# Layer two's first-mixer GELUs of tiles 4 to 11 in the tanh form, ranks and rates set anew, and queues left in the planner's order, in a two-layer attention and mixer kernel

## The chip, the cores and the metric

The kernel runs on one core of a Trainium2 chip. Times are device microseconds of that core. The time before is 1024.59 us, the median of three runs (1024.34 to 1025.14). TensorE (PE), VectorE (DVE), ScalarE (ACT), GpSimd (POOL) and the DMA queue of SyncE (SP) each work through a list of instructions in a fixed order and wait for each other by semaphores.

## The reference

The input is 2048 rows of 448 numbers, in bfloat16. Block A is attention with 16 heads of 28 dimensions, block B a token-shifting mixer and an MLP. Each stands behind a layer norm, and the pair runs twice with the same weights (cut to what matters):

```
def _A_ref(x, wqkv, wo):
    qkv = (x @ wqkv) split into q, k, v of 16 heads
    p = softmax(q @ k^T * 28 ** -0.5)
    return (p @ v) @ wo
def _B_ref(x, w1, w2, w3, w4):
    h = gelu_tanh(layernorm(x) @ w1)
    hs = (h, its quarters shifted by 1, -1, 2, -2 rows) @ w2
    x1 = x + hs
    return x1 + gelu_tanh(layernorm(x1) @ w3) @ w4
x = x + A(layernorm(x)); x = x + B(layernorm(x))
x = x + A(layernorm(x)); x = x + B(layernorm(x))
```

## The kernel before

**Tiles and chunks.** The 2048 rows are 16 tiles of 128. For queries, a layer has five chunks: tiles 0-3, 4-7, 8-11, 12-13 and 14-15. The heads are worked four at a time, in four groups. The MLP of block B runs over five groups of tiles: 0-2, 3-6, 7-10, 11-12 and 13-15.

**The stream of exponentials.** `t_scores` (L1775) writes score blocks of 128 keys by 512 (or two of 256) into PSUM with L1654. Two or three blocks make a unit; units take turns on banks 0-2 and 3-4, so PE can be two units ahead of ACT. `t_exp` (L1877) turns a whole unit into probabilities by one ACTIVATE of 1536 or 1024 columns (L1892), and `t_pv` (L1904) multiplies them with v (L1050). A share of the blocks doesn't go to ACT: `d_first` and `d_chain` (L1734, L1747) compute the exponential on DVE with five instructions (L1736, L1763, L1765, L1767, L1770). `R_RATE` and `D_RATE` say how large this share is in each stretch.

**The first mixer.** `t_mixA` (L2093) multiplies a chunk with w1, and DVE brings its four groups into `hT` (L2128). Its GELU is done in one of two forms. In the tanh form (`tanh_gelu`, L2152) each group takes a square (L2156, on POOL or DVE), a product on DVE (L2157), a Tanh of 512 columns on ACT (L2158) and a second product on DVE (L2159). In the wide form one ACTIVATE with the GELU function takes all four groups at once (L2140, 2048 columns). The table `PAIR` chooses the wide form for a chunk and names the group of tiles with whose MLP GELU (`t_mixB`, L2339) it shares a stay of ACT in the GELU table. Both then wait for each other:

```
PAIR = {(0, 12): 7, (1, 4): 0, (1, 8): 3}
...
once = (L, tiles[0]) in PAIR and not direct
...
for f in range(14):
    yield ("wait", ("h2", L, PAIR[L, t0], f))
...
for (L_, c0), g0 in sorted(PAIR.items()):
    if (L_, g0) == (L, tiles[0]) and not direct:
        for grp in range(4):
            yield ("wait", ("hz", L, c0, grp))
```

**Who sets the order.** All of this is written as generators that offer operations to a planner (`Sched.run`, L618). It holds a cost for each operation, chooses what an engine takes next by readiness and by `RANK`, and puts dummy matmuls on the identity (L2385) into PE's gaps. `WIN`, `TARGET` and `LWIN` say how densely, and `W_POS` and `Q_LEAD` when weights and queries are loaded. The result is one list for each engine. In the kernel before, this list isn't the last word: `Plan.rearranged` (L274) takes 370 pairs from `MOVES` (L19), each of which puts one operation behind another on the same engine, and `WEAVE` (L67) says how the five lists are interleaved for the recording of dependences. `FILL_MORE` (L172) lengthens six stretches of dummy matmuls.

**Start and end.** Before the first score, PE transposes the normalised tiles 0 to 3 (L1283, recorded as `ps<-ident,xn`), DVE copies them (L1290), and PE projects keys and queries (L1059). Beside it ACT packs weights (L1188) and squares them (L1200); PE sums those squares (L1050 on `ones_bf`) for the bound under the softmax. After the last exponential, what remains is the MLP of tiles 7 to 15 and the last chunk's mixer, and the GELUs then come straight out of PSUM (L2313, L2123).

Of the kernel before, what the change touches and what calls it, by code (L numbers as in the profile page):

```python
# [2496 lines left out]
```

## Time and profile before

| | |
|---|---|
| median of three runs | 1024.59 us (1024.34 to 1025.14) |
| span of the profiled execution, first to last instruction | 1022.4 us, its clock 1.000 |
| ACT busy | 981.4 us, 894 instructions |
| PE busy, and of that dummy matmuls on the identity | 973.8 us, 150.1 us (3524 of 16283) |
| DVE busy | 811.0 us |
| POOL busy | 292.3 us |
| ACT table loads | 14 of 1.283 us |

The span leaves out what lies before the first and behind the last instruction; to the median of the runs it is 2.2 us. Busy time on PE overlaps (four matmuls run side by side in column groups, their ends are modelled), and successive ACTIVATEs overlap by a little, so the cost of one on ACT is the distance to the start of the next rather than its own length.

### The profile page before, as it was taken

The page shows a single profiled execution, that of the slowest core. Times are in us where ns is not written, and L with a number is a line of the kernel's source. Part 1 is how long each engine was busy: PE and PEld are TensorE (multiplying, and loading weights), DVE is VectorE, ACT ScalarE, POOL GpSimd, SP SyncE. Part 2 cuts the span into 40 slices and gives each one's busy share as a digit, 9 for nine tenths or more (in the row PEclk, how much of TensorE's full clock was granted, in tenths as well). Part 3 has the DMA queues.
Part 4 walks back from the last instruction along what each step waited for, and adds up shares of the span by engine and source line. Part 5 has one row for each costly group of instructions (what it writes and reads, how often), then busy time and mean ns, then how long its engine had stood idle before and what let it go on. Part 6 is the DMA issues. An engine that isn't in the chain of part 4 may idle for free.

```text
span 1022.4 us, 36170 instructions
## 1 busy us (share of the span) xinstructions
PE 973.8 (95%) x16283; PEld 412.9 (40%) x16285; DVE 811.0 (79%) x1572; ACT 981.4 (96%) x894; POOL 292.3 (29%) x462
## 2 busy tenths in 40 slices
PE   8999999999999999999999999999999999999998
PEld 4332443443433254333433443433433433454565
DVE  8777999989888958876877868688898589866651
ACT  8999999999999999999999999999999999999942
POOL 3312021531453016252325112012624120532230
PEclk9999999999999999999999999999999999999999
DMA  4643413320321013131131024423302020121101
GB/s 126 161 111 117 119 45 79 53 39 23 76 61 28 13 37 96 23 48 34 48 111 38 33 69 134 141 66 99 65 25 37 17 68 16 31 57 31 26 12 33
DMA packets 99394, 62.57 MB, mean 61 GB/s; under 512 B 68712, under 2 KB 88552, under 8 KB 99240
## 3 DMA queue, kind: packets, MB, share of 16 engines
q1 hardware_dynamic: 99240, 60.27, 23.6%
q8 instruction: 127, 2.08, 0.9%
q14 instruction: 27, 0.22, 0.1%
HBM read 28.16 MB, written 16.76 MB: 44 GB/s over the span
## 4 chain that ended last, share of the span: by engine, by line
ACT 71%; PE 23%; DVE 4%; DMA 1%; issue 1%; DVEq 0%
ACT PT L1892 65%; PE ps L1059 14%; PE ps L1654 5%; PE ps L1050 4%; ACT h2T L2339 2%; ACT fb L2158 1%; PE ps L2385 1%; ACT L1892 1%; DVE PD L1770 0%; ACT hT L2140 0%; DVE h2T L2317 0%; DMA xT<-xn 0%; ACT L2339 0%; DMA obf<-in_A_x_dram 0%; DVE yd L1736 0%
## 5 line engine op out<-in xcount | busy, mean ns | idle before, releaser
L1892 ACT ACTIVATE PT<-ps 128x1024 bf16<-128x1024 f32 (+1 forms) x782 | 887.3, 1333 | 2.9 <-PE ps L1654 2.1
L1654 PE MATMUL ps<-qT,kT 32*128 32x512 bf16 (+1 forms) x2304 | 269.8, 335 | 24.2 <-ACT PT L1892 18.4
L1050 PE MATMUL ps<-PT,vaug 128*32 128x512 bf16 (+1 forms) x2420 | 246.1, 341 | 0.7 <-ACT PT L1892 0.2
L1059 PE MATMUL ps<-xT,w 128*32 128x512 bf16 (+4 forms) x2656 | 177.9, 344 | 4.2 <-DVE h2T L2317 2.2
L1654 PEld LDWEIGHTS ps<-qT,kT 32*128 32x128 bf16 x2304 | 69.7, 91 | 256.0 <-ACT PT L1892 227.0
L2385 PE MATMUL ps<-ident 128*32 128x256 bf16 x3524 | 150.1, 276 | 1.8 <-POOL ident L1144 1.5
L2385 PEld LDWEIGHTS ps<-ident 128*32 128x32 bf16 x3524 | 98.9, 97 | 28.5 <-issue 11.9
L1050 PEld LDWEIGHTS ps<-PT,vaug 128*32 128x32 bf16 x2420 | 74.0, 95 | 89.4 <-issue 71.0
L1999 POOL TENSOR_TENSOR otn<-ub,fb 128x512 bf16<-128x512 f32 (+1 forms) x31 | 34.7, 1120 | 210.3 <-DMA fb<-rscr 202.9
L1736 DVE TENSOR_SCALAR yd<-ps 128x512 int32<-128x512 f32 x109 | 74.6, 685 | 22.8 <-PE ps L1654 21.7
L1059 PEld LDWEIGHTS ps<-xT,w 128*32 128x32 bf16 (+1 forms) x2656 | 69.2, 95 | 56.7 <-issue 25.0
L1763 DVE SCALAR_TENSOR_TENSOR fb<-yd 128x512 f32<-128x512 uint16 x109 | 78.5, 724 | 0.8
L1765 DVE SCALAR_TENSOR_TENSOR fb<-fb,yd 128x512 f32<-128x512 f32 x109 | 77.9, 717 | 0.7
L1770 DVE SCALAR_TENSOR_TENSOR PD<-yd,PD 128x512 int16<-128x512 int16 x109 | 75.9, 698 | 1.6
L1059 PE MATMUL ps<-w,h2T 128*32 128x448 bf16 x1120 | 75.4, 355 | 1.1 <-ACT h2T L2339 1.0
L2317 DVE CAST h2T<-ps 128x512 bf16<-128x512 f32 (+1 forms) x70 | 44.4, 635 | 16.2 <-PE ps L1059 15.0
L1392 POOL TENSOR_TENSOR sq<-qT 128x512 bf16<-128x512 bf16 x24 | 28.5, 1190 | 96.2 <-DVE qT L1451 93.4
L1392 POOL TENSOR_TENSOR sq<-kT 128x512 bf16<-128x512 bf16 (+2 forms) x32 | 30.4, 950 | 83.0 <-DVE kT L1406 79.9
L1767 DVE TENSOR_SCALAR PD<-fb 128x512 bf16<-128x512 f32 x109 | 49.6, 456 | 1.0
L1059 PE MATMUL ps<-xT,wk_pad 128*32 128x512 bf16 (+2 forms) x576 | 47.6, 359 | 0.7 <-DVE kT L1406 0.3
L1654 PE MATMUL ps<-wk_pad,kT 32*128 32x512 bf16 x256 | 39.6, 384 | 4.6 <-ACT PT L1892 4.0
L1059 PE MATMUL ps<-xT,wq_pad 128*32 128x512 bf16 x512 | 43.2, 382 | 0.5 <-issue 0.5
(189 smaller groups left out, 1195.9 us busy)
## 6 DMA issues: line engine op xcount, KB each, us to landing
uscr<-ub SPq DMA_DIRECT2D x28, 256.0 KB
ub<-uscr SPq DMA_DIRECT2D x28, 256.0 KB, 6.8
fb<-rscr SPq DMA_DIRECT2D x24, 256.0 KB
xnd<-xn SPq DMA_DIRECT2D x28, 128.0 KB, 2.3
xd<-x_res SPq DMA_DIRECT2D x16, 224.0 KB, 2.1
x_res<-xd SPq DMA_DIRECT2D x16, 224.0 KB, 4.2
w<-in_B_w_dram SPq DMA_DIRECT2D x5, 448.0 KB, 6.0
obf<-in_A_x_dram SPq DMA_DIRECT2D x16, 112.0 KB
```

Of the source, the lines that this page charges most:

```text
L1050: return lambda e: e.matmul(out=out, lhsT=lhsT, rhs=rhs, start=start, stop=stop, **kw)
L1059: r.append(e.matmul(out=out[c:c + w, :], lhsT=lhsT[:, c:c + w], rhs=rhs, start=start, stop=stop, tile_position=(0, c)))
L1392: return both("sq", 0.15 + NW * 0.0018, 0.07 + NW * 0.00104, lambda e: e.tensor_tensor(out=sq[:, si, 0:NW], in0=src, in1=src, op=ALU.mult) ...
L1654: yield op("pe", (0.005 + NW * 0.00042) / nc_, lambda e, i=i, kc=kc, j=j, g=g, qt=qt, a=a, NW=NW, bank=bank: e.matmul(out=ps[:, bank, i * ...
L1736: yield op("dve", c_ps(512), lambda e: e.tensor_scalar(out=y, in0=ps[:, bi(bank), :], scalar1=SCALE * L2E * FS, scalar2=-126.0 * FS, op0=A ...
L1763: yield op(D_[0][0], D_[0][1], lambda e: e.scalar_tensor_tensor(out=q, in0=lo, scalar=E2 / E3 * FS, in1=lo, op0=ALU.add, op1=ALU.mult), re ...
L1765: yield op(D_[1][0], D_[1][1], lambda e: e.scalar_tensor_tensor(out=q, in0=q, scalar=E1 / E3 * FS * FS, in1=lo, op0=ALU.add, op1=ALU.mult) ...
L1767: yield op(D_[2][0], D_[2][1], lambda e: e.tensor_scalar(out=pdt, in0=q, scalar1=E3 / FS ** 3, scalar2=E0, op0=ALU.mult, op1=ALU.add), rea ...
L1770: yield op(D_[3][0], D_[3][1], lambda e: e.scalar_tensor_tensor(out=pdt.bitcast(I16), in0=hi, scalar=128.0, in1=pdt.bitcast(I16), op0=ALU. ...
L1892: yield op("act", 0.069 + n * w * 0.000833, lambda e, bk=bk, s0=s0, n=n, w=w: e.activation(out=PT[:, s0:s0 + n, 0:w], in_=ps[:, bk[0]:bk[0 ...
L2317: ev = op("dve", c_ps(m * NW), lambda e, hr=hr, pv=pv: e.tensor_copy(out=hr, in_=pv), reads=[("ps", bi(b))], writes=hk, touch=[b])
L2385: return [e.matmul(out=ps[32 * c:32 * c + 32, bi(b), 0:256].rearrange("p (a n) -> p a n", n=128), lhsT=ident[:, 32 * c:32 * c + 32], rhs=i ...
```

## The change

`MOVES`, `WEAVE` and `FILL_MORE` become empty, so each engine gets its instructions in the order of the planner. `PAIR` loses its two entries of layer two: chunks 4-7 and 8-11 take the tanh form, and the wide GELUs of the groups of tiles 0-2 and 3-6 wait for them no more. The planner's other tables get new numbers.

```
-MOVES = (
-    (94, 115), (95, 94), (96, 95), (97, 96), (125, 118), (128, 125), (130, 134), (238, 231), (244, 238), (245, 244),
...
-WEAVE = (
-    "vdvvvvsgdvgvvdtgtvgdtvtgdtsgtgvdvtvttdvtvvtdttvtvdgtgtdvtvtdtstvvtdgsvtttdtsgtttttstttsvttttvstgtttttttvtttttt",
...
-FILL_MORE = (
-    (2714, 4), (2725, 9), (3749, 15), (5548, 4), (5564, 4), (9810, 14),
-)
+MOVES = ()
+WEAVE = ()
+
+FILL_MORE = ()
...
-DPRIO = 3.5
+DPRIO = 4.797
...
-RHI = 7
+RHI = 9
...
-DTH = 0.4
-XSHUT = (8, 83)
+DTH = 0.396
+XSHUT = (10, 78)
...
-DDTH = 1.3
+DDTH = 1.889
...
-Q_LEAD = {(0, 0): 0, (0, 1): 4, (0, 2): 45, (0, 3): 11, (1, 0): 18, (1, 1): 12, (1, 2): 4, (1, 3): 26}
+Q_LEAD = {(0, 0): 0, (0, 1): 8, (0, 2): 54, (0, 3): 11, (1, 0): 7, (1, 1): 17, (1, 2): 8, (1, 3): 35}
...
-Sched.TARGET = 0.695
+Sched.TARGET = 0.78
 Sched.LOW = 0
-Sched.WIN = 1.582
-Sched.LWIN = 3.6
+Sched.WIN = 1.535
+Sched.LWIN = 3.231
...
-W_POS = (6, 9, 17, 5, 5, 5, 25, 21)
-V_FIRST = 1.366
-K_FIRST = (0.756, 0.932, 1.363)
-Q_FIRST = (0.531, 1.956, 2.405)
+W_POS = (3, 7, 17, 5, 3, 14, 29, 16)
+V_FIRST = 1.113
+K_FIRST = (0.617, 0.789, 1.032)
+Q_FIRST = (0.3, 1.262, 2.77)
...
-PAIR = {(0, 12): 7, (1, 4): 0, (1, 8): 3}
+PAIR = {(0, 12): 7}
```

`RANK`, `R_RATE`, `D_RATE` and `PE_NORM` change in the same way, number by number. What this makes of the built program, counted in it:

| | before | changed |
|---|---|---|
| exponentials on ACT (L1892), and blocks of 512 columns in them | 782, 1938 | 781, 1940 |
| exponentials on DVE, chains of five | 110 | 108 |
| GELU of 2048 columns (L2140) | 2 | 0 |
| Tanh of 512 columns of the first mixer (L2158 on `hT`) | 16 | 24 |
| products of the tanh form on DVE, 512 columns (L2157 and L2159 on `hT`) | 16 and 16 | 24 and 24 |
| squares of the tanh form, 512 columns (L2156 on `hT`), DVE and POOL | 5 and 11 | 10 and 14 |
| ACT table loads | 14 | 14 |
| dummy matmuls on the identity | 3524 | 3652 |

More of the change, by code (lines that the diff above doesn't have):

```diff
@@ L172 @@
-FILL_MORE = (
-    (2714, 4), (2725, 9), (3749, 15), (5548, 4), (5564, 4), (9810, 14),
-)
+MOVES = ()
+WEAVE = ()
+FILL_MORE = ()
 class _Op:
@@ L771 @@
 PVB = 2
-DPRIO = 3.5
+DPRIO = 4.797
 DST = [('dve', 0.6), ('dve', 0.6), ('dve', 0.34), ('dve', 0.6)]
 DSEG = 1
-R_RATE = {0: 0.072, 1: 0.054, 2: 0.185, 3: 0.027, 4: 0.084, 5: 0.015, 6: 0.079, 7: 0.153, 8: 0.15, 9: 0.2, 10: 0.068, 11: 0.141, 13: 0.013, 14: 0.093, 15: 0.07, 16: 0.166, 17: 0.069, 18: 0.125, 19: 0.035, 20: 0.104, 21: 0.101, 22: 0.2, 24: 0.083, 25: 0.131, 26: 0.05, 27: 0.2, 28: 0.031, 29: 0.146, 30: 0.13, 31: 0.151, 32: 0.106, 34: 0.194, 35: 0.032, 36: 0.048, 37: 0.159, 38: 0.2, 39: 0.152, 40: 0.017, 41: 0.066, 42: 0.126, 43: 0.193, 44: 0.161, 45: 0.152, 46: 0.185, 47: 0.071, 48: 0.099, 49: 0.145, 50: 0.04, 51: 0.149, 52: 0.2, 53: 0.035, 54: 0.081, 55: 0.109, 56: 0.113, 57: 0.2, 58: 0.094, 59: 0.173, 60: 0.07, 61: 0.036, 62: 0.03, 63: 0.022}
+R_RATE = {0: 0.033, 1: 0.054, 2: 0.181, 3: 0.053, 4: 0.132, 5: 0.035, 6: 0.019, 7: 0.153, 8: 0.189, 9: 0.2, 10: 0.068, 11: 0.076, 13: 0.052, 14: 0.093, 15: 0.07, 17: 0.183, 18: 0.2, 19: 0.035, 20: 0.156, 22: 0.2, 24: 0.189, 27: 0.198, 28: 0.031, 29: 0.159, 30: 0.051, 31: 0.121, 32: 0.091, 34: 0.2, 37: 0.11, 38: 0.044, 39: 0.188, 40: 0.017, 42: 0.126, 43: 0.078, 44: 0.155, 46: 0.2, 47: 0.059, 48: 0.099, 49: 0.145, 50: 0.04, 52: 0.2, 53: 0.025, 54: 0.081, 55: 0.113, 56: 0.128, 57: 0.078, 59: 0.042, 60: 0.07, 61: 0.067, 62: 0.035, 63: 0.022, 12: 0.017, 23: 0.166, 41: 0.019, 25: 0.031}
 RLO = 5
-RHI = 7
+RHI = 9
 RPRIO = 1
 DWIN = 2
-DTH = 0.4
-XSHUT = (8, 83)
+DTH = 0.396
+XSHUT = (10, 78)
 DLO = 6
@@ L784 @@
 DPK = 2
-DDTH = 1.3
+DDTH = 1.889
 UPRIO = 2
 UWAIT = 1
-RANK = {('q', 0, 1): 1.458, ('q', 0, 2): 3.2, ('q', 0, 3): 2.4, ('q', 1, 0): 2.293, ('q', 1, 1): 2.021, ('q', 1, 2): 3.05, ('q', 1, 3): 1.801, ('b', 0, 0): 2.202, ('b', 0, 1): 3.2, ('b', 0, 2): 2.582, ('b', 0, 3): 3.2, ('b', 0, 4): 1, ('b', 1, 0): 2.957, ('b', 1, 1): 2.988, ('b', 1, 2): 3.1, ('b', 1, 3): 2.326, ('b', 1, 4): 2.625, ('a', 0, 0): 1, ('a', 0, 1): 1.329, ('a', 0, 2): 2.222, ('a', 0, 3): 1.987, ('a', 0, 4): 1.487, ('a', 1, 0): 2.563, ('a', 1, 1): 2.326, ('a', 1, 2): 1, ('a', 1, 3): 1.418, ('a', 1, 4): 1.12, ('k', 0, 1): 2.363, ('k', 0, 2): 3.2, ('k', 0, 3): 3.2, ('k', 1, 0): 2.011, ('k', 1, 1): 2.88, ('k', 1, 2): 2.852, ('k', 1, 3): 2.609, ('k', 1, 4): 1, ('c', 0, 0): 1, ('c', 0, 1): 2.803, ('c', 0, 2): 1.953, ('c', 0, 3): 1.333, ('c', 0, 4): 2.22, ('c', 1, 0): 2.575, ('c', 1, 1): 2.272, ('c', 1, 2): 2.13, ('c', 1, 3): 1, ('c', 1, 4): 1, ('w', 0, 0): 3.2, ('w', 0, 1): 2.902, ('w', 0, 2): 1.222, ('w', 0, 3): 2.911, ('w', 0, 4): 2.596, ('w', 1, 0): 2.665, ('w', 1, 1): 3.2, ('w', 1, 2): 3.125, ('w', 1, 3): 3.2, ('w', 1, 4): 2.29, ('o', 0, 0): 1.812, ('o', 0, 1): 1.176, ('o', 0, 2): 1.382, ('o', 0, 3): 3.2, ('o', 0, 4): 1, ('o', 1, 0): 2.392, ('o', 1, 1): 3.077, ('o', 1, 2): 1.372, ('o', 1, 3): 1.772, ('o', 1, 4): 1.234, ('v', 0, 1): 2.98, ('v', 0, 2): 1.671, ('v', 0, 3): 3.2, ('v', 1, 0): 1.713, ('v', 1, 1): 2.534, ('v', 1, 2): 2.146, ('v', 1, 3): 2.138, ('v', 1, 4): 3.2, ('l', 1, 0): 2.708, ('l', 1, 1): 2.19, ('l', 1, 2): 1.408, ('l', 1, 3): 3.2, ('l', 1, 4): 2.671, ('t', 0, 0): 2.601, ('t', 0, 1): 2.03, ('t', 0, 2): 2.728, ('t', 0, 3): 3.07, ('t', 0, 4): 2.082, ('t', 1, 0): 1.898, ('t', 1, 1): 2.494, ('t', 1, 2): 2.877, ('t', 1, 3): 2.854, ('t', 1, 4): 1, ('m', 0, 0): 1, ('m', 0, 1): 1.667, ('m', 0, 2): 2.633, ('m', 0, 3): 2.857, ('m', 0, 4): 1.917, ('m', 1, 0): 2.491, ('m', 1, 1): 2.982, ('m', 1, 2): 1.289, ('m', 1, 3): 2.323, ('m', 1, 4): 2.62, ('e', 0, 0): 0.6, ('e', 0, 1): 0.666, ('e', 0, 2): 1.865, ('e', 0, 3): 1.412, ('e', 0, 4): 0.716, ('e', 1, 0): 0.703, ('e', 1, 1): 2.839, ('e', 1, 2): 0.6, ('e', 1, 3): 0.722, ('e', 1, 4): 0.679, ('n', 0, 0): 1.011, ('n', 0, 1): 1.107, ('n', 0, 2): 1.382, ('n', 0, 3): 1.706, ('n', 0, 4): 1.167, ('n', 1, 0): 0.6, ('n', 1, 1): 1.548, ('n', 1, 2): 1.666, ('n', 1, 3): 1.653, ('n', 1, 4): 1.663}
@@ L789 @@
-Q_LEAD = {(0, 0): 0, (0, 1): 4, (0, 2): 45, (0, 3): 11, (1, 0): 18, (1, 1): 12, (1, 2): 4, (1, 3): 26}
-D_RATE = {1: 0.194, 3: 0.3, 4: 0.033, 6: 0.118, 7: 0.195, 8: 0.122, 9: 0.124, 10: 0.166, 11: 0.072, 12: 0.023, 13: 0.025, 14: 0.281, 15: 0.015, 16: 0.293, 17: 0.033, 18: 0.288, 19: 0.106, 20: 0.056, 21: 0.3, 22: 0.057, 23: 0.097, 24: 0.185, 25: 0.22, 26: 0.255, 27: 0.117, 28: 0.3, 29: 0.081, 30: 0.058, 32: 0.151, 33: 0.011, 34: 0.268, 35: 0.165, 37: 0.3, 38: 0.218, 39: 0.061, 40: 0.025, 41: 0.299, 42: 0.272, 43: 0.122, 44: 0.137, 45: 0.032, 46: 0.014, 47: 0.256, 48: 0.021, 49: 0.021, 50: 0.107, 51: 0.074, 52: 0.129, 54: 0.155, 55: 0.3, 56: 0.3, 57: 0.162, 58: 0.227, 59: 0.149, 60: 0.061, 61: 0.154, 62: 0.079, 63: 0.137}
@@ L791 @@
-PE_NORM = {(0, 0): 0, (0, 1): 0, (0, 2): 0, (0, 3): 0, (0, 4): 0, (1, 0): 0, (1, 1): 0, (1, 2): 0, (1, 3): 0, (1, 4): 1}
+RANK = {('q', 0, 1): 1.529, ('q', 0, 2): 3.2, ('q', 0, 3): 2.4, ('q', 1, 0): 2.293, ('q', 1, 1): 1.947, ('q', 1, 2): 3.05, ('q', 1, 3): 1.147, ('b', 0, 0): 2.071, ('b', 0, 1): 3.2, ('b', 0, 2): 2.649, ('b', 0, 3): 3.061, ('b', 0, 4): 1, ('b', 1, 0): 1.526, ('b', 1, 1): 2.988, ('b', 1, 2): 2.904, ('b', 1, 3): 2.119, ('b', 1, 4): 2.559, ('a', 0, 0): 1, ('a', 0, 1): 1.329, ('a', 0, 2): 3.102, ('a', 0, 3): 2.09, ('a', 0, 4): 1.56, ('a', 1, 0): 1.126, ('a', 1, 1): 1.363, ('a', 1, 2): 2.002, ('a', 1, 3): 2.451, ('a', 1, 4): 2.131, ('k', 0, 1): 2.252, ('k', 0, 2): 3.031, ('k', 0, 3): 3.2, ('k', 1, 0): 2.054, ('k', 1, 1): 2.905, ('k', 1, 2): 2.853, ('k', 1, 3): 2.609, ('k', 1, 4): 1, ('c', 0, 0): 1, ('c', 0, 1): 3.043, ('c', 0, 2): 1.986, ('c', 0, 3): 2.534, ('c', 0, 4): 2.249, ('c', 1, 0): 2.575, ('c', 1, 1): 2.044, ('c', 1, 2): 1.058, ('c', 1, 3): 1.094, ('c', 1, 4): 2.116, ('w', 0, 0): 1.569, ('w', 0, 1): 2.708, ('w', 0, 2): 1.222, ('w', 0, 3): 2.916, ('w', 0, 4): 2.085, ('w', 1, 0): 2.665, ('w', 1, 1): 2.176, ('w', 1, 2): 2.488, ('w', 1, 3): 3.2, ('w', 1, 4): 1.727, ('o', 0, 0): 1.814, ('o', 0, 1): 1.459, ('o', 0, 2): 1.07, ('o', 0, 3): 3.2, ('o', 0, 4): 1, ('o', 1, 0): 1.731, ('o', 1, 1): 3.012, ('o', 1, 2): 1.574, ('o', 1, 3): 2.146, ('o', 1, 4): 1, ('v', 0, 1): 2.98, ('v', 0, 2): 1.671, ('v', 0, 3): 3.2, ('v', 1, 0): 1.981, ('v', 1, 1): 2.421, ('v', 1, 2): 2.144, ('v', 1, 3): 1.392, ('v', 1, 4): 2.544, ('l', 1, 0): 2.708, ('l', 1, 1): 2.342, ('l', 1, 2): 1.152, ('l', 1, 3): 3.087, ('l', 1, 4): 1.775, ('t', 0, 0): 3.183, ('t', 0, 1): 2.03, ('t', 0, 2): 2.728, ('t', 0, 3): 3.024, ('t', 0, 4): 2.654, ('t', 1, 0): 2.807, ('t', 1, 1): 2.762, ('t', 1, 2): 3.151, ('t', 1, 3): 3.099, ('t', 1, 4): 2.905, ('m', 0, 0): 1, ('m', 0, 1): 1, ('m', 0, 2): 2.363, ('m', 0, 3): 3.156, ('m', 0, 4): 2.922, ('m', 1, 0): 2.491, ('m', 1, 1): 3.076, ('m', 1, 2): 2.965, ('m', 1, 3): 2.551, ('m', 1, 4): 3.051, ('e', 0, 0): 0.6, ('e', 0, 1): 0.783, ('e', 0, 2): 1.865, ('e', 0, 3): 1.464, ('e', 0, 4): 0.734, ('e', 1, 0): 0.703, ('e', 1, 1): 2.839, ('e', 1, 2): 2.154, ('e', 1, 3): 0.919, ('e', 1, 4): 0.6, ('n', 0, 0): 1.115, ('n', 0, 1): 1.448, ('n', 0, 2): 1.476, ('n', 0, 3): 1.706, ('n', 0, 4): 1.117, ('n', 1, 0): 0.694, ('n', 1, 1): 1.555, ('n', 1, 2): 1.698, ('n', 1, 3): 1.629, ('n', 1, 4): 1.621}
@@ new lines @@
+Q_LEAD = {(0, 0): 0, (0, 1): 8, (0, 2): 54, (0, 3): 11, (1, 0): 7, (1, 1): 17, (1, 2): 8, (1, 3): 35}
+D_RATE = {1: 0.194, 3: 0.3, 6: 0.118, 7: 0.143, 8: 0.18, 9: 0.124, 10: 0.237, 11: 0.072, 13: 0.025, 14: 0.3, 16: 0.206, 18: 0.288, 20: 0.056, 21: 0.255, 22: 0.131, 23: 0.2, 24: 0.194, 25: 0.22, 26: 0.143, 27: 0.15, 28: 0.045, 29: 0.074, 30: 0.041, 32: 0.151, 33: 0.216, 35: 0.022, 37: 0.3, 38: 0.062, 39: 0.061, 40: 0.025, 41: 0.206, 42: 0.3, 43: 0.093, 44: 0.163, 46: 0.014, 47: 0.03, 48: 0.021, 49: 0.021, 50: 0.107, 51: 0.074, 52: 0.213, 54: 0.155, 55: 0.245, 56: 0.3, 57: 0.179, 58: 0.228, 59: 0.149, 60: 0.057, 61: 0.133, 62: 0.157, 63: 0.145, 5: 0.093, 19: 0.03, 53: 0.279}
@@ L792 @@
+PE_NORM = {(0, 0): 0, (0, 1): 0, (0, 2): 0, (0, 3): 0, (0, 4): 0, (1, 0): 0, (1, 1): 0, (1, 2): 0, (1, 3): 0, (1, 4): 2}
 TANHW = {(0, 0): 0, (0, 3): 0, (0, 7): 0, (0, 11): 1, (0, 13): 0, (1, 0): 0, (1, 3): 0, (1, 7): 0, (1, 11): 0, (1, 13): 0}
 Sched.AGED = 0
-Sched.TARGET = 0.695
+Sched.TARGET = 0.78
 Sched.LOW = 0
-Sched.WIN = 1.582
-Sched.LWIN = 3.6
+Sched.WIN = 1.535
+Sched.LWIN = 3.231
 GSL = 0
@@ L814 @@
 COLD = 6.0
-Sched.DOUBT2 = {"dma": 1.5, "pool": 0.2, "dve": 0.5, "act": 0.5, "pe": 0.0}
+Sched.DOUBT2 = {'dma': 1.5, 'pool': 0.2, 'dve': 0.5, 'act': 0.5, 'pe': 0}
 Sched.EARLY = 0.1
-Sched.DOUBT = {"dma": 0.8, "pool": 0.6, "dve": 0.05, "act": 0.05}
+Sched.DOUBT = {'dma': 0.8, 'pool': 0.6, 'dve': 0.05, 'act': 0.05}
+Sched.LCRED = 0.3
 def PENORM(L, ch, g):
```

102 lines of the change are left out of this document (removed), and 45 rows, old and new, of the table MOVES.

## The prediction

> **What bounds the kernel now.** I read the page first, then the chain of waits, then busy time by stage.
>
> ```profile
> span 1022.4 us, 36170 instructions
> PE 973.8 (95%) x16283; PEld 412.9 (40%) x16285; DVE 811.0 (79%) x1572; ACT 981.4 (96%) x894; POOL 292.3 (29%) x462
> ACT 71%; PE 23%; DVE 4%; DMA 1%; issue 1%; DVEq 0%
> ```
>
> Two engines look full. Which one sets the end depends on the stage, so the next view gives busy time in five windows of us; the first number after each is its length, and the brackets count instructions.
>
> ```profile
> 27.00:968.00 941.00, 898.86 (x14709) 369.15 (x14709) 768.67 (x1454) 937.16 (x833) 275.95 (x421) 1.00 0.25 62
> 666.00:760.00 94.00, 89.34 (x1386) 35.62 (x1382) 80.96 (x139) 93.35 (x88) 30.07 (x41) 1.00 0.27 66
> 760.00:830.00 70.00, 66.20 (x1045) 26.84 (x1045) 53.45 (x106) 69.72 (x59) 24.40 (x45) 1.00 0.18 37
> 830.00:968.00 138.00, 132.82 (x2465) 60.68 (x2468) 107.76 (x210) 136.70 (x120) 35.69 (x62) 1.00 0.15 36
> 968.00:1022.00 54.00, 51.45 (x1194) 32.81 (x1182) 19.41 (x39) 20.50 (x34) 8.19 (x20) 1.00 0.07 22
> ```
>
> Columns are PE, PEld, DVE, ACT, POOL, then granted clock. From 27 to 968 us ACT works 937.16 of 941: 3.84 us idle is all that a better order could still win there, and each us of ACT work or idle added lengthens the run. Behind 968, the last exponential, PE works 51.45 of 54 and ACT waits. What keeps ACT fed is seen in the waits (us in total, times, longest):
>
> ```profile
> PEld ps L1654 <- ACT PT L1892: 258.8, 668, 2.0
> ...
> ACT PT L1892 <- PE ps L1654: 2.1, 4, 1.1
> ...
> ACT fb L2158 <- DVE fb L2157: 0.7, 1, 0.7
> ```
>
> PE is early for the scores 668 times, by 258.8/668 = 0.39 us on average; that is the cover under every PE stall. It was bare four times, and a bare one cost 2.1/4 = 0.5 us.
>
> **The change part by part.** Counted in the built programs, the planner's list hardly changes up to about 666 us: PE's order in the changed one differs at 51 places from the old kernel's list without `MOVES`, but at 169 from the old kernel as it ran. So two thirds of the run get the old plan back with its rearrangement undone; only behind 666 us is the plan new.
>
> *The head.* Here the undone moves can be costed. In the new PE list the four matmuls that sum the squared key weights stand behind the first of the second eight transposes; before, they stood behind all eight.
>
> ```profile
> 7.81 1.41 DVE L1290 COPY xT<-ps 128x512 bf16<-128x512 bf16 x4
> 7.94 0.62 PE L1283 MATMUL ps<-ident,xn 128*128 128x128 bf16 x8
> 8.06 0.62 ACT L1200 ACTIVATE PT<-wk_pad 128x512 bf16<-128x512 bf16 x1
> 8.94 0.25 PE L1050 MATMUL ps<-ones_bf,PT 128*128 128x1 bf16 x4
> 9.46 0.60 PE L1059 MATMUL ps<-xT,wk_pad 128*32 128x512 bf16 x8
> 15.21 2.37 ACT L1892 ACTIVATE PT<-ps 128x1536 bf16<-128x1536 f32 x2
> ```
>
> The squares end at 8.06 + 0.62 = 8.68. The sum started 0.26 later, so seven transposes come behind 8.94 rather than before 7.94 + 0.62 = 8.56. They end near 9.6, about 1.05 behind the 8.56 of before, and so do DVE's last two copies, which the key projection at 9.46 waited for. Queued behind it are the score bound and the first exponential at 15.21. POOL's 1 us power in between may hide part: +1.0 us, bounds 0.5 and 1.2.
>
> *ACT's own work.* Removed are two GELUs of 2048 columns, added are eight Tanhs of 512. From start to next start:
>
> ```profile
> 205.45 0.81 ACT L2158 ACTIVATE fb<-fb 112x512 f32<-112x512 f32 x1
> 205.97 2.54 ACT L1892 ACTIVATE PT<-ps 128x1536 bf16<-128x1536 f32 x2
> 807.63 1.91 ACT L2140 ACTIVATE hT<-hT 112x2048 bf16<-112x2048 bf16 x1
> 809.45 2.43 ACT L2339 ACTIVATE vaug<-vaug 128x2688 bf16<-128x2688 bf16 x1
> 899.97 1.90 ACT L2140 ACTIVATE hT<-hT 112x2048 bf16<-112x2048 bf16 x1
> 901.89 1.28 ACT L1892 ACT_TABLE_LOAD   x1
> 615.31 50.79 ACT PT L1892 x45
> ```
>
> A Tanh takes 0.52 and needs no table load before the exponential behind it; the GELUs took 1.82 and 1.92. That is 8 x 0.52 - 3.74 = +0.42. No table load goes: the partner's GELU stays, 14 loads before and after. ACT also gets two blocks more (1940 for 1938, as DVE computes 108 for 110). The chain's piece above holds 45 exponentials of 2.5 blocks: 50.79/112.5 = 0.45 a block, +0.90. Together +1.3.
>
> *DVE and POOL.* Sixteen products at about 0.69 and five squares on DVE, three on POOL, less two chains of five. The windows of 666 to 830 leave DVE 94 + 70 - 134.4 = 29.6 us, so the work has room. What isn't sure is when each Tanh finds its input:
>
> ```profile
> 745.17 0.69 DVE L2157 SCALAR_TENSOR_TENSOR fb<-fb,hT 112x512 f32<-112x512 f32 x1
> 750.41 1.48 POOL L1999 TENSOR_TENSOR otn<-ub,fb 128x512 bf16<-128x512 f32 x1 [9.98 <-DMA fb<-rscr]
> 750.67 1.76 DVE L2157 SCALAR_TENSOR_TENSOR fb<-fb,hT 112x512 f32<-112x512 f32 x1
> 752.47 0.63 ACT L2158 ACTIVATE fb<-fb 112x512 f32<-112x512 f32 x1 [0.65 <-DVE fb L2157]
> ```
>
> The product takes 0.69, but the one that began under POOL's multiplication took 1.76 and ended 0.54 behind it; the Tanh came late and ACT stood 0.65, with the exponentials, and the PE scores that need their banks, queued behind. This is one of four Tanhs of layer two's first chunk, so eight new ones give 2 x 0.65 = 1.3 at that rate; of all 16 Tanhs of 512 columns it is the only one that waited for its product (the third row of the waits), so at that rate 0.3. I take +0.6, bounds 0 and 8 x 0.65 = 5.2. [...]
>
> *The tail.* Behind the last score PE has 36 fewer matmuls of 512 columns (w3, tiles 7-10), 16 more of 256 and 5 more with v.
>
> ```profile
> 963.62 0.62 PE L1059 MATMUL ps<-xT,w 128*32 128x512 bf16 x8
> 964.53 0.40 PE L1059 MATMUL ps<-xT,w 128*32 128x512 bf16 x4
> 966.76 0.62 PE L1059 MATMUL ps<-xT,w 128*32 128x256 bf16 x16 [0.21 <-DMA xT<-xn]
> 967.63 0.95 PE L1059 MATMUL ps<-xT,w 128*32 128x256 bf16 x28
> ```
>
> By the differences one of 512 costs 0.22/4 = 0.055 and one of 256 costs 0.33/12 = 0.0275: -36 x 0.055 + 16 x 0.0275 + 5 x 0.0275 = -1.4.
>
> *The other undone moves and the new numbers.* `MOVES` left PE's list different from the plan at 202 places, mostly a few matmuls with v set behind one or two score groups. No row shows the unmoved list. From below: the cover of 0.39 takes every stall, 0. From above: one place in ten bare at 0.5, 10 us. ACT's idle of 3.84 us in 941 is a list out of which such places had been taken, so some come back; I take one in twenty, +5.0. Weight loads (`W_POS`) and POOL's and SP's orders I cost at nothing: DMA holds 1% of the chain. If a load came late, the price would be in the same 0 to 10.
>
> Sum: 1.0 + 1.3 + 0.6 - 1.4 + 5.0 = +6.5. The span goes from 1022.4 to 1028.9; the median stood 2.2 above the span, so 1031.1 us.
>
> **The rivals.**
> 1. *The cover takes it all.* Places and Tanhs cost nothing: 1.0 + 1.3 - 1.4 = +0.9, 1025.5 us. For it: the 0.39 us at 668 groups. Against: the head, where a move of the same kind was worth 1 us.
> 2. [...] 6.5 - 0.6 + 5.2 = +11.1, 1035.7 us. For it: the 1.76 row. Against: one late Tanh in 16.
> 3. *PE's clock falls.* Six lengthened stretches of dummies are gone; during the first wide GELU 240 dummies become 208.
>
> ```profile
> 360.71 6.73 PE L2385 MATMUL ps<-ident 128*32 128x256 bf16 x240
> 367.88 2.46 PE L1059 MATMUL ps<-w,h2T 128*32 128x448 bf16 x48 [0.43 <-ACT h2T L2339]
> ```
>
> At 6.73/240 = 0.028 each the 208 last 5.8, and PE stands 7.17 - 5.8 = 1.3 us. Suppose PE then ran at half speed for as long as that stretch lasted, 7.17 us: it would fall 3.6 behind, less 0.39 of cover at each of some six units, so 1.2; at six places 7.2 on the sum, 1038.3 us. Against: the granted clock was 1.00 in every window, and the changed list holds more dummies in all. [...]
> 4. *Faster: the new plan behind 666 us packs ACT without idle.* Place: 666 to 968 us, where ACT idles 0.65 + 0.28 + 1.30 = 2.2. With the two wide GELUs no longer waiting for chunks 4-7 and 8-11, these gaps close: 1025.5 - 2.2 = 1023.3; it becomes faster than now by over 0.2% once a further 0.8 us of the first 639 us' 1.6 idle goes or the head hides half its delay. Against: that needs an unmoved list tighter than a moved one.
>
> **How the numbers follow.** Forecast 0.57 (its own range 1026.7 to 1036), rivals 0.15, 0.12, 0.06 and 0.10. About 2 us (0.2%) is what a measurement of this kernel tells from no change, so same is 1022.5 to 1026.6. Faster is 0.06 of rival 4, past the point named. Same is its other 0.04 and 0.11 of rival 1, which lies 1.1 under the edge: 0.15. The rest is slower, 0.79. The range is 1024.0 to 1039.0, leaving out rival 4's lower end and the upper tail of undone places.
>
> **What would show it.** Head: the first exponential near 16.2. ACT between first and last exponential: idle near 9 us instead of 4, its waits for L1654 many more than 4 times; 24 Tanhs of 0.52. Tail: about 1.4 shorter from last exponential to end. Granted clock 1.00. The forecast is wrong if ACT's idle there stays under 5 us, or if a stretch behind 666 us holds over half of the loss.

## The result, and the profile after

The changed kernel takes 1030.53 us (median of four runs, 1028.56 to 1031.92); the kernel before took 1024.46 beside it. The ratio is 1.0059, its 95% interval 1.0045 to 1.0073. The forecast was 1031.1, slower.

The page of the changed kernel, its totals and the row of the granted clock in 40 slices of 25.8 us:

```profile
span 1030.2 us, 36436 instructions
PE 982.9 (95%) x16411; PEld 418.3 (41%) x16413; DVE 830.9 (81%) x1584; ACT 983.2 (95%) x897; POOL 301.0 (29%) x466
PEclk9999999999999999999999999989999999989999
ACT 72%; PE 21%; DVE 5%; POOL 1%; issue 1%; DMA 0%; SPq 0%; DVEq 0%; ACTq 0%
```

The chain is the same mixture as before. New are the two slices in which the clock is under 0.9. The busy time by stage shows the rest. First the kernel before, from its first exponential to the end of its last, its part behind 666 us, and what follows the last; then the same three rows of the changed kernel (length, the busy time of PE, PEld, DVE, ACT and POOL, the granted clock, then DMA's share and GB/s):

```profile
15.21:968.33 953.12, 909.94 (x14875) 373.23 (x14879) 780.12 (x1482) 949.24 (x845) 278.82 (x424) 1.00 0.25 61
666.00:968.36 302.36, 288.72 (x4900) 123.48 (x4900) 242.16 (x454) 300.11 (x267) 90.16 (x147) 1.00 0.19 46
968.33:1022.40 54.07, 51.12 (x1182) 32.49 (x1170) 19.41 (x39) 20.17 (x34) 8.19 (x20) 1.00 0.07 22
```

```profile
15.71:977.68 961.97, 920.90 (x15032) 379.88 (x15032) 800.66 (x1495) 951.48 (x850) 286.27 (x427) 0.99 0.24 61
666.00:977.68 311.68, 295.95 (x4924) 124.77 (x4922) 260.09 (x469) 304.81 (x272) 95.74 (x151) 0.98 0.19 46
977.68:1030.20 52.52, 49.59 (x1146) 31.32 (x1141) 18.70 (x38) 19.87 (x31) 9.40 (x21) 1.00 0.07 22
```

The whole difference of 7.8 us between the two profiled executions is in these rows. The first exponential starts 0.50 later (15.71 for 15.21). ACT works 951.48 - 949.24 = 2.24 longer. ACT stands idle 961.97 - 951.48 = 10.49 instead of 3.88, so 6.61 longer. The tail is 1.55 shorter. 0.50 + 2.24 + 6.61 - 1.55 = 7.80. Behind 666 us alone, ACT's idle time went from 2.25 to 6.87. This execution was the longest of the four. The median run is 1.4 us shorter; which part of the loss is smaller in it isn't shown, as only this execution has a trace.

ACT's waits (us in total, times, longest) say for whom it stood; no Tanh is among them:

```profile
ACT PT L1741 <- PE ps L1503: 8.6, 10, 3.1
ACT PT L1741 <- PE ps L899: 0.8, 1, 0.8
```

Ten waits for scores instead of four. Only three places make up most of it: near 110 us (0.52), 681 to 689 us (0.76, 1.35 and 0.17) and 922 to 926 us (3.10, 0.27 and 0.93), together 7.10. In steps of 3 us, PE and its clock at the first and the last of these:

```profile
103.00:106.00 3.00, 2.23 (x22) 0.61 (x21) 2.89 (x15) 3.00 (x3) 0.00 (x0) 1.00 0.54 158
106.00:109.00 3.00, 2.59 (x26) 0.80 (x28) 2.33 (x4) 3.00 (x4) 1.04 (x1) 0.60 0.00 0
...
916.00:919.00 3.00, 1.37 (x28) 0.54 (x26) 3.00 (x4) 2.96 (x3) 1.92 (x2) 0.99 0.29 50
919.00:922.00 3.00, 2.22 (x38) 1.15 (x42) 2.71 (x6) 0.00 (x0) 1.22 (x2) 0.50 0.65 191
922.00:925.00 3.00, 3.00 (x53) 1.45 (x50) 1.54 (x3) 2.47 (x2) 0.91 (x2) 0.50 0.01 1
925.00:928.00 3.00, 3.00 (x74) 1.59 (x74) 2.24 (x5) 2.28 (x2) 1.14 (x1) 0.87 0.26 49
```

Each time PE rests first, and then its granted clock falls to one half for some microseconds: in steps of 1 us it is 0.50 from 107 to 110, from 681 to 686 and from 919 to 925. The rests don't have one cause. Near 105 us PE's timeline has three short ones (0.47, 0.30 and 0.41), all of them waits for ACT to free a bank for the next scores: PE is early there and has few dummies. Near 678 there are two, one for ACT (0.58) and one for a late sum of DVE (1.05). (At 680 us the rows are alike: PE busy 2.00 of 3.00 from 679 to 682, then clock 0.50.) Why PE rested at 917 us is in the timelines of DVE, POOL, PE and ACT (start, length, idle time before it and who ended it):

```profile
914.05 1.32 DVE L1113 TENSOR_SCALAR xn<-x1b,mv,mst 128x448 bf16<-128x448 f32 x1 [0.77 <-POOL mst L2082]
915.29 3.17 DVE L1614 SCALAR_TENSOR_TENSOR fb<-fb,yd 128x512 f32<-128x512 f32 x2
918.39 0.75 DVE L1616 TENSOR_SCALAR PD<-fb 128x512 bf16<-128x512 f32 x2
919.06 0.67 DVE L2076 SCALAR_TENSOR_TENSOR x1b<-x_res,mst,ps 128x448 f32<-128x448 f32 x1
913.98 3.93 POOL L2091 TENSOR_TENSOR x_res<-x_res,x1b 128x448 f32<-128x448 f32 x3
917.08 0.29 PE L2234 MATMUL ps<-ident 128*32 128x256 bf16 x4
919.78 1.69 PE L2234 MATMUL ps<-ident 128*32 128x256 bf16 x28 [2.41 <-DVE x1b L2076]
922.06 1.45 ACT L1741 ACTIVATE PT<-ps 128x1536 bf16<-128x1536 f32 x1 [3.10 <-PE ps L1503]
923.77 1.02 ACT L1741 ACTIVATE PT<-ps 128x1024 bf16<-128x1024 f32 x1 [0.27 <-PE ps L1503]
925.72 2.36 ACT L1741 ACTIVATE PT<-ps 128x1536 bf16<-128x1536 f32 x2 [0.93 <-PE ps L1503]
```

Three additions of POOL run from 913.98 to 917.91. Beside them two products of DVE, which begin at 915.29, take 3.17. DVE's sum `x1b` stands behind them and ends at 919.73. PE's next dummy matmuls write the bank that this sum reads, so they wait 2.41, with the scores behind them; and those 28 dummies, and the scores after them, then run at half clock (0.50; 1.69 us for the 28, where 28 others took 0.95 at 912.57). ACT stands 4.30 in all. The forecast had looked for such a late product at the Tanhs; it came at DVE's own exponentials.

### The profile page after: what moved, and what is told of

Its sections match the earlier page's. It is cut to its first block, busy times and chain, and to the rows that moved or that the text cites. A ratio compares the mean times of both kernels' runs of the same rounds, so it can differ in the third digit from the quotient of the medians.

```text
span 1030.2 us, 36436 instructions
## 1 busy us (share of the span) xinstructions
PE 982.9 (95%) x16411; PEld 418.3 (41%) x16413; DVE 830.9 (81%) x1584; ACT 983.2 (95%) x897; POOL 301.0 (29%) x466
## 4 chain that ended last, share of the span: by engine, by line
ACT 72%; PE 21%; DVE 5%; POOL 1%; issue 1%; DMA 0%; SPq 0%; DVEq 0%; ACTq 0%
ACT PT L1741 65%; PE ps L908 11%; PE ps L1503 5%; PE ps L899 3%; ACT h2T L2188 3%; PE ps L2234 2%; ACT fb L2007 1%; DVE fb L1614 1%; ACT L1741 1%; ACT L2188 1%; DVE PD L1619 1%; DVE yd L1585 0%; DVE fb L1612 0%; DMA PT<-in_A_wqkv_dram 0%; DVE qT L1300 0%
## 5 line engine op out<-in xcount | busy, mean ns | idle before, releaser
L908 PE MATMUL ps<-xT,w 128*32 128x512 bf16 (+4 forms) x2656 | 186.1, 345 | 3.4 <-DVE h2T L2166 2.6
L2234 PE MATMUL ps<-ident 128*32 128x256 bf16 x3652 | 163.9, 279 | 4.7 <-DVE x1b L2076 2.4
L2234 PEld LDWEIGHTS ps<-ident 128*32 128x32 bf16 x3652 | 105.9, 98 | 35.6 <-issue 12.5
L1616 DVE TENSOR_SCALAR PD<-fb 128x512 bf16<-128x512 f32 x107 | 47.4, 444 | 1.1
L908 PE MATMUL ps<-xT,wq_pad 128*32 128x512 bf16 x512 | 45.4, 395 | 1.2 <-DVE qT L1300 0.6
```

The costliest lines, as they stand in the source:

```text
L908: r.append(e.matmul(out=out[c:c + w, :], lhsT=lhsT[:, c:c + w], rhs=rhs, start=start, stop=stop, tile_position=(0, c)))
L1616: yield op(D_[2][0], D_[2][1], lambda e: e.tensor_scalar(out=pdt, in0=q, scalar1=E3 / FS ** 3, scalar2=E0, op0=ALU.mult, op1=ALU.add), rea ...
L2234: return [e.matmul(out=ps[32 * c:32 * c + 32, bi(b), 0:256].rearrange("p (a n) -> p a n", n=128), lhsT=ident[:, 32 * c:32 * c + 32], rhs=i ...
```

## The experiments

Times stand beside runs of the kernel before on the same chip. "Idle" is ACT's between the first and the end of the last exponential, in the profiled execution (before 3.88, changed 10.49). Where `MOVES` or `FILL_MORE` is used without a `WEAVE`, the interleaving for the recording is worked out from what each operation reads and writes. `head_undone` shows that this costs nothing that can be measured: it differs from the kernel before in that and in four pairs, and its ratio is 1.0005.

| run | median, us | ratio to before, 95% interval | idle | runs at clock 1.000 |
|---|---|---|---|---|
| changed kernel | 1030.53 | 1.0059 [1.0045, 1.0073] | 10.49 | 0 of 4 |
| moves_undone | 1028.03 | 1.0035 [1.0022, 1.0048] | 4.08 | 3 of 7 |
| moves_undone_tanh | 1027.71 | 1.0036 [1.0024, 1.0048] | 5.67 | 1 of 5 |
| new_numbers_wide | 1033.47 | 1.0102 [1.0084, 1.0121] | 7.42 | 0 of 6 |
| head_undone | 1024.37 | 1.0005 [0.9996, 1.0013] | 3.03 | 10 of 11 |
| fill_918 | 1028.49 | 1.0039 [1.0026, 1.0052] | 6.58 | 1 of 5 |
| pool_later | 1025.73 | 1.0015 [1.0007, 1.0024] | 5.11 | 3 of 11 |
| mended | 1025.52 | 1.0011 [1.0002, 1.0020] | 4.19 | 6 of 11 |
| dummies_thinned | 1028.63 | 1.0047 [1.0031, 1.0062] | 6.16 | 0 of 4 |
| undone_dummies_kept | 1028.21 | 1.0038 [1.0025, 1.0050] | 7.00 | 4 of 11 |
| order_restored | 1023.15 | 0.9991 [0.9979, 1.0002] | 3.22 | 7 of 12 |
| order_restored_2 | 1022.75 | 0.9993 [0.9984, 1.0002] | 2.12 | 8 of 11 |

### The three parts of the change

`moves_undone` is the kernel before with

```
-MOVES = ( ...
-WEAVE = ( ...
-FILL_MORE = ( ...
+MOVES = ()
+WEAVE = ()
+FILL_MORE = ()
```

> The kernel before with only the rearrangement, the recording order and the lengthened dummies taken out (old numbers, old table of wide GELUs). Theory A, the forecast's: the loss of the change is the undone order, spread thinly over PE's 202 places, each a bare wait without a clock fall; then this kernel alone is +4 to +8 us on the kernel before (1028.5 to 1032.5), with ACT idle near 9 us in waits for scores that are all under 1.2 us. Theory B: the loss sits in three pauses of PE of the new plan (near 106, 680 and 918 us of the changed kernel) after which PE's granted clock shows 0.50; two of them lie behind 666 us, which the old plan doesn't share, so this kernel is +1 to +3 (1025.5 to 1027.5): head 0.5, the first 639 us 1.2 more idle, nothing else.

`moves_undone_tanh` is that, with

```
-PAIR = {(0, 12): 7, (1, 4): 0, (1, 8): 3}
+PAIR = {(0, 12): 7}
```

> As the kernel with only the order undone, and the two layer-two entries of the table of wide GELUs taken out besides (tanh form, old numbers). If the form by itself costs what the forecast put on it (+0.4 ACT work, -1.4 tail, Tanhs late 0 to 5.2), it lies within 1 us of that kernel where no Tanh is late. Rival: the tanh form's extra products on DVE make DVE late for PE, PE pauses for over 1 us and its clock falls: +3 us or more on that kernel, with windows of clock 0.50.

`new_numbers_wide` is the changed kernel with this line the other way round.

> The changed kernel with the two wide GELUs of layer two put back, its new numbers and planner's order kept. If the new numbers carry the loss, it stays within 1.5 us of the changed kernel (1029 to 1032). If the tanh form carries it, it falls by 3 us or more, to 1027.5 or less. Both may shift by the plan's luck behind 666 us; the trace's pauses of PE and windows of clock under 0.95 say which.

The undone order alone costs 0.35%, 3.6 us. The tanh form adds nothing to it (1.0036 for 1.0035). With the new numbers, the tanh form is worth 4.4 us (1.0059 for 1.0102), and `new_numbers_wide` came out above both of its expected ranges. On the old plan the same form changed nothing, so the difference is put down to the plan that the planner falls into; no run separates the two. The plan with the wide form has a tail of 58.05 us, 4 longer than the kernel before:

```profile
16.23:974.35 958.12, 918.11 (x15146) 383.21 (x15145) 780.94 (x1467) 950.70 (x845) 282.10 (x422) 0.99 0.24 61
974.35:1032.40 58.05, 55.06 (x1258) 35.58 (x1248) 20.47 (x41) 21.17 (x37) 8.83 (x22) 1.00 0.08 23
```

On the undone order neither theory holds as it stood. Its profiled execution had a full clock and stood at 1025.78:

```profile
15.88:969.85 953.97, 908.25 (x14708) 369.30 (x14710) 779.40 (x1482) 949.89 (x845) 280.70 (x424) 1.00 0.24 61
```

ACT's idle time there is 953.97 - 949.89 = 4.08, only 0.2 more than before. 202 places of PE's list had been put back, and in this execution ACT waited for PE seven times, for 2.8 us in all, where the kernel before waited four times for 2.1: theory A's 9 us weren't there. Yet its seven runs spread from 1025.05 to 1030.69, and the three with a mean clock of 1.000 took 1025.05, 1025.78 and 1028.03, the one with 0.995 took 1030.69. The spread is larger than theory B gave it, too.

### The head

`head_undone` takes four of the 370 pairs out of the kernel before, those that put the sums of squared key weights behind the transposes.

```
-    (94, 115), (95, 94), (96, 95), (97, 96), (125, 118), ...
+    (125, 118), ...
```

> The kernel before with only four of its pairs taken out, those that put the four sums of squared key weights behind all eight transposes. The forecast's head term: +1.0 (0.5 to 1.2), first exponential at 16.2. By the changed kernel's trace, whose first exponential came at 15.71: +0.5. If the stream of exponentials took it up later: 0.

The first exponential came at 15.73 instead of 15.21, +0.52. So by the trace it is +0.5, not 1.0. The time rose by 0.05%, with an interval of -0.04% to +0.13%, which can't tell 0, 0.5 and 1.0 us apart. These are the rows of this run:

```profile
7.89 0.23 PE L1222 MATMUL ps<-ident,xn 128*128 128x128 bf16 x1
8.68 0.25 PE L989 MATMUL ps<-ones_bf,PT 128*128 128x1 bf16 x4 [0.56 <-ACT PT L1139]
8.79 0.55 PE L1222 MATMUL ps<-ident,xn 128*128 128x128 bf16 x7
```

The sums start at 8.68, right behind the squares. The 0.26 that the forecast put between the two was PE's dummies of the kernel before, which stood ahead of the sums, not the way from ACT to PE. The transposes therefore end at 9.34 and not at 9.6.

### The pause at 917 us

`fill_918` lengthens one step of four dummies, the one at 917.08, which writes a free bank. DVE and POOL are untouched.

```
+FILL_MORE = ((10060, 18),)
```

> The changed kernel; one dummy step at 917.08 us (4 matmuls) becomes 72 in the same free bank, so that PE works through its pause of 2.41 us there; the late product of DVE that the next dummies wait for is left late. Theory B (pause, then half clock): the granted clock behind 918 us shows 1.00, the first bare wait of ACT falls from 3.10 to near 2.1 us (DVE's product ends at 919.73, then 28 dummies 0.8, scores 0.4) and the two behind it (0.27, 0.93) vanish: -2 us at this place. Rival: the clock has no part in it, the bare waits come from the late product alone: 4.30 us of bare waits in 920 to 927 stay within 0.3.

```profile
913.37 3.18 DVE L1656 SCALAR_TENSOR_TENSOR fb<-fb,yd 128x512 f32<-128x512 f32 x2
915.16 2.15 PE L2276 MATMUL ps<-ident 128*32 128x256 bf16 x72
917.86 0.95 PE L2276 MATMUL ps<-ident 128*32 128x256 bf16 x28 [0.56 <-DVE x1b L2118]
919.18 1.45 ACT L1783 ACTIVATE PT<-ps 128x1536 bf16<-128x1536 f32 x1 [2.15 <-PE ps L1545]
920.79 10.28 ACT L1783 ACTIVATE PT<-ps 128x1024 bf16<-128x1024 f32 x9 [0.15 <-PE ps L1545]
```

The timelines of this run (1.9 us earlier here, line numbers 42 higher): DVE is as late as before, 3.18. But PE is busy through the pause, the 28 dummies take 0.95 instead of 1.69, and ACT stands 2.15 + 0.15 = 2.30 instead of 4.30. The granted clock was 1.00 in each step of 3 us from 916 to 925. So of the 4.30, 2.0 came from the clock, as theory B gave it; the rest is the late sum. The other places were left as they were, and the one run whose mean clock was 1.000 took 1028.49, no less than the others (1027.47 to 1029.06), so what is left of the loss isn't the clock alone.

`pool_later` leaves PE and DVE as they were and puts two of POOL's three additions behind the next power on POOL:

```
+MOVES = ((10032, 10080), (10035, 10032),)
```

> The changed kernel; on POOL alone, two of three residual additions at 914 to 918 us stand behind the next power instead of ahead of it, no instruction more or less. Theory P (DVE and POOL shut each other out): DVE's two products at 915.29 take 1.2 instead of 3.17 us, the product that PE waits for ends near 918 instead of 919.7, PE's pause falls under 0.8 us, no window behind 918 shows a clock under 0.95 and ACT's bare waits in 918 to 927 fall from 4.3 to under 1 us: -3 to -4 us in all, on the profile's place. Rival: DVE's row is long for another reason, nothing moves: bare waits there stay above 3.5 us.

```profile
911.73 1.14 POOL L2133 TENSOR_TENSOR x_res<-x_res,x1b 128x448 f32<-128x448 f32 x1
913.04 1.28 DVE L1656 SCALAR_TENSOR_TENSOR fb<-fb,yd 128x512 f32<-128x512 f32 x2
914.91 0.67 DVE L2118 SCALAR_TENSOR_TENSOR x1b<-x_res,mst,ps 128x448 f32<-128x448 f32 x1
918.04 2.23 POOL L2133 TENSOR_TENSOR x_res<-x_res,x1b 128x448 f32<-128x448 f32 x2
916.96 1.45 ACT L1783 ACTIVATE PT<-ps 128x1536 bf16<-128x1536 f32 x1 [0.26 <-PE ps L1545]
```

The same two products take 1.28 instead of 3.17; nothing of them was changed but what POOL does meanwhile. ACT stands 0.26 there and 0.15 at the next unit, 0.41 instead of 4.30, and the median falls from 1.0059 to 1.0015 of the kernel before. Two instructions on an engine that is busy 29% of the time, standing about 5 us too early, made about 4.5 of the 6 us by the medians, whose intervals leave some 1.5 us either way, and 3.9 at this place in the traces. `fill_918` is the control: its recording is worked out in the same way, POOL's three additions stay together in it, and the products take 3.18. The falls of the clock also differ from execution to execution: the profiled one of `pool_later` has one between 760 and 830 us (a mean clock of 0.98 over that window; ACT stood 0.80 ahead of 767.25), where that of the changed kernel has none (1.00).

`mended` adds two things more: DVE's sum that PE waited for at 680 us goes ahead of three steps of a DVE exponential, and eight dummies more near 105 us.

```
+MOVES = ((7396, 7379), (10032, 10080), (10035, 10032),)
+FILL_MORE = ((1046, 3),)
```

> The changed kernel with all three places mended: POOL's two additions later (at 914), DVE's addition that PE waits for at 680 moved ahead of three steps of a DVE exponential, and 8 more dummies at 104.9. If the three pauses with their fall of the clock carry the loss against the order-undone kernel, the median comes to 1025.5 to 1027.5 with a granted clock of 0.998 or more. If the loss is spread thinly, it gains 1 us or less: 1029.5 or more.

1025.52, as theory B had it, but hardly below the run before. At 680 us only the name of the late product changed: PE no longer waits for L1371 (which was L1329), but the next product in DVE's queue is late now.

```profile
678.43 0.74 DVE L1866 SCALAR_TENSOR_TENSOR ub<-ub,fct,ps 128x512 f32<-128x512 f32 x1
679.22 0.45 PE L941 MATMUL ps<-PD,vaug 128*32 128x512 bf16 x1 [1.03 <-DVE ub L1866]
```

PE rests 1.03, where it had rested 1.05, and the window from 680 to 685 shows a clock of 0.72.

Part of why DVE is late here stands 4 us ahead of it, and it looks like what happened at 914 us:

```profile
674.55 1.15 POOL L1283 TENSOR_TENSOR sq<-qT 128x512 bf16<-128x512 bf16 x1 [2.07 <-DVE qT L1342]
674.72 1.53 DVE L1656 SCALAR_TENSOR_TENSOR fb<-fb,yd 128x512 f32<-128x512 f32 x1
```

A product of the same form takes 0.68 at 670.90. The one that began 0.17 behind a square of POOL took 1.53, and DVE then worked without a gap up to the product that PE waited for. The changed kernel has the same pair of rows at 676 (1.15 and 1.53). So at two of the three places a product of DVE is long beside POOL; here it is 0.85 longer, ahead of a rest of 1.03. No run moved this square, so that it is the cause here isn't shown.

### How long a rest lowers the clock

`dummies_thinned` is the kernel before in its own order; in four stretches under a GELU the last dummies become one matmul of 32 by 8 columns each.

```
+THIN = ((3749, 3752), (6538, 6559), (8705, 8733), (9784, 9810))
```

> The kernel before (its order as it ran); in four stretches of dummies under the wide GELUs the last dummies are shrunk to one matmul of 32 by 8 columns, so that PE has almost nothing to do for about 2.4 us (near 365), 2.6 (597), 3.4 (807) and 4.9 (895) before its next real matmuls. Asked: from which pause on the granted clock falls, and what a fall costs. Theory B, from the three falls of the changed kernel: a pause of 2.4 us already brings a window of about 0.50 that lasts 3 to 7 us, at all four places, and each costs 1 to 4 us: 1028 to 1040. [...]

The windows behind the four rests, and for the last also those in it:

```profile
368.20:373.00 4.80, 4.75 (x98) 2.39 (x102) 1.43 (x3) 4.77 (x4) 0.22 (x1) 1.00 0.19 72
600.50:605.00 4.50, 3.90 (x72) 1.82 (x75) 2.17 (x4) 4.47 (x6) 0.00 (x0) 1.00 0.03 8
811.20:816.00 4.80, 4.19 (x80) 1.89 (x80) 3.68 (x8) 4.78 (x4) 0.78 (x2) 1.00 0.01 3
894.00:900.00 6.00, 3.69 (x128) 3.19 (x122) 4.61 (x9) 5.99 (x2) 0.00 (x0) 0.91 0.07 22
900.00:904.00 4.00, 2.51 (x28) 1.12 (x32) 0.24 (x2) 3.98 (x3) 0.73 (x1) 0.50 0.04 10
904.00:908.00 4.00, 4.00 (x67) 1.71 (x62) 1.55 (x4) 2.90 (x3) 0.19 (x1) 0.78 0.00 0
```

In this execution only the longest rest (3.80 behind 1.14 of small matmuls) had a fall of the clock with it, to 0.50; behind it ACT stood 1.49. The three shorter (1.98, 1.96 and 1.59, behind 0.6 to 0.9 of small matmuls) had none: the clock behind them is 1.00. Theory B's "all four places" isn't what the profiled execution shows. The three other runs had mean clocks of 0.992 and 0.993, where this one had 0.997, so in them more was lost than one such fall; where, no trace says. A fixed bound of rest isn't shown either, and the busy share of PE in a few microseconds doesn't decide it: PE was busy 1.11 of 3.00 us from 597.5 to 600.5 here and the clock stayed at 1.00, while 2.23 of 3.00 from 103 to 106 in the changed kernel had a fall behind it.

### Putting the order back

`undone_dummies_kept` is `moves_undone` with the old `FILL_MORE` kept.

> The kernel before without its rearrangement, but with its six lengthened stretches of dummies kept. Theory B (what the undone order loses, it loses by falls of the clock, since its profiled run with a granted clock of 1.000 stood only 1.7 us above the kernel before while its seven runs spread from 1025.05 to 1030.69): if those falls come where the dummies are missing, this kernel holds 1.000 in most runs and comes to 1025 to 1026.5. Rival: the falls come at pauses elsewhere, where no dummies stand (near 106 us), and the six stretches change nothing: 1027 to 1028.5, with clocks of 0.995 to 0.998 in half of the runs. Theory A (thin loss in bare places): the same 1027 to 1028.5, but at clock 1.000.

No gain: 1.0038 for 1.0035. The missing long stretches of dummies weren't what cost time in the undone order. Its profiled run has a fall near 452 us (0.66 from 450 to 455), where none of the six stretches is, with bare waits of 1.12, 0.22 and 0.29. The four runs at 1.000 still took 1026.8 to 1028.2, so most of the undone order's price there isn't the clock. The kernel before isn't free of falls either: of its 22 runs beside this one, three had a mean clock of 0.997 or 0.998 and took 1026.53 to 1028.89, the others 1022.87 to 1024.73.

`order_restored` puts 230 of the old pairs back into the changed kernel, those up to 655 us whose two operations the new plan has at the same place, and keeps two of the three mended places in this form; the eight dummies near 105 us are left out:

```
+MOVES = ( ... 230 pairs ...
+    (7396, 7379), (7385, 7404), (10032, 10080), (10035, 10032),)
```

> The changed kernel with 230 of the old pairs put back for the first 655 us (those whose two operations the new plan has at the same place) and three mended places behind it (POOL's two additions at 914 later; at 680 DVE's addition for PE ahead of one step). Theory B: the tail's 1.5 us of gain remains, the head's 0.5 us is back, the pauses at 106, 680 and 918 are gone or short: 1022 to 1024, at or under the kernel before, with clock 0.998 or more. If the tanh form and the new numbers cost by themselves what the forecast put on them (+1.3 of ACT work with no gain elsewhere), it ends at 1024.5 to 1026.

1023.15, 0.9991 of the kernel before. From `mended` it is 0.2%, 2.0 us: that is what the pairs for the first 655 us, with one more step of DVE at 680 and without the eight dummies, are worth in this plan. By their ratios, each good to 0.1 or 0.2%, the runs thus account for the loss: 0.44% for POOL's two additions, 0.04% for the two other mended places, 0.20% for the old order of the first 655 us, which holds the head's 0.5 us too. With all of this mended, the tanh form, the new numbers and the shorter tail together cost nothing that can be measured.

`order_restored_2` mends two bare waits that the profile of `order_restored` showed:

```
+    (1066, 1060), (1067, 1066), (7698, 7703), (7699, 7698),
+FILL_MORE = ((1046, 3),)
```

> The changed kernel with the restored order, and two places more, named by the profile of that kernel: at 104 us eight more dummies and two matmuls with v ahead of a score group (there PE rested three times for 1.1 us in all, ran at clock 0.66 behind it, and ACT stood 0.50), and at 707 us one score group ahead of an output projection that waits for a late product (ACT stood 0.51). Theory B: both bare waits go, -0.5 to -1.0 us: 1022.2 to 1022.7, an interval wholly below the kernel before. Rival: the rests at 104 are too short to matter and the fall there was chance, the ACT wait at 707 only moves: 1023.0 to 1023.4.

Both waits are gone from the profiled execution, and it holds the full clock:

```profile
15.13:967.52 952.39, 912.50 (x15041) 377.66 (x15040) 794.92 (x1495) 950.27 (x850) 285.68 (x427) 1.00 0.24 61
```

952.39 - 950.27 = 2.12 us idle, the least of all runs, with 1.0 us more of ACT work than the kernel before and a tail 1.6 shorter. The median of 1022.75 is far under the changed kernel. Against the kernel before beside it, though, its ratio is 0.9993, no better than the 0.9991 of `order_restored`, so a gain from the two waits isn't shown. The expected interval wholly below the kernel before was missed: this one (0.9984 to 1.0002) and that of `order_restored` (0.9979 to 1.0002) just reach 1, so that either is faster is likely, but not shown. Its eight runs at clock 1.000 took 1022.06 to 1023.06, its three at 0.998 took 1024.11 to 1024.50. The two groups lie about 1.8 us apart; the slower one has no trace.

## Why the number was right and its places wrong

The forecast said slower, by a sum of +6.5; the median says +6.1, the profiled execution +7.8. That the sum came so near is luck in its largest term, which was a chosen rate between 0 and 10 us and stood for something other than what happened. By its terms:

- **Head**, +1.0: measured +0.50, the lower bound. The direction and the mechanism were right; the step "the sum started 0.26 later" took dummies ahead of the sum for the way from ACT to PE.
- **ACT's work**, +1.3: measured +2.24 in the profiled execution, +1.6 in those of `pool_later` and `mended`, which do the same ACT work (950.87 and 950.89). Right, a little small.
- **Tanhs late**, +0.6: 0. None of the Tanhs waited in the profiled execution. The rival that gave this 5.2 us is out.
- **Tail**, -1.4: measured -1.55. But it isn't the tanh form's own gift: with the old numbers and the tanh form the tail was 55.47, longer than before.
- **Other undone moves and new numbers**, +5.0: with the idle time that the Tanhs were to bring, 5.6; measured +6.61 of ACT idle. The size was right, the picture wrong. One place in twenty, bare at 0.5, means ten small waits all over the run. There were three places: 7.10 us in 106 to 110, 680 to 689 and 918 to 926. The forecast had named what would refute it, a stretch behind 666 us with over half of the loss: ACT's idle there rose by 4.62, of 7.8. That is the step that failed, and it failed because the term was a rate without a place: it priced every undone place alike, and most of what was lost hung on what DVE and POOL were doing at one place.
- **The clock**, a rival at 0.06, 1.00 in the forecast itself: it fell at three places. The rival had the course of it, PE rests and then runs at half speed (0.50 at all three) with ACT bare behind it, but tied it to the rest under the first wide GELU. That rest was there, 1.30 us as worked out, and the clock stayed 1.00:

```profile
363.69 5.86 PE L2234 MATMUL ps<-ident 128*32 128x256 bf16 x208
370.85 1.50 PE L908 MATMUL ps<-w,h2T 128*32 128x448 bf16 x25 [1.30 <-ACT h2T L2188]
```

What made PE rest instead was a late sum of DVE at 917 us, another together with a wait for ACT near 680, and waits for ACT alone near 105. The forecast had quoted a product of DVE that took 1.76 us beside POOL instead of 0.69, and asked of it only whether a Tanh would be late. Had it asked who else stands behind such a product, it would have come to PE's banks.

Shown by a run that changes that alone: POOL's two additions as the cause at 914 us, 3.9 us in the traces and about 4.5 of the 6 by the medians; the clock as 2.0 of the 4.30 us there; the head's 0.5, by the trace. Not shown: what the long product at 676 us costs; what makes the undone order with the old numbers 3.6 us slower where its profiled execution stood 1.9 us above the kernel before; and why the fall near 106 us comes in some executions (the changed kernel, `fill_918`, `order_restored`) and not in others with the same order on PE there (`pool_later`).
